# Low halves of converted float64 weights: from GpSimd to VectorE, in one operation with the factor

## The chip, the cores and the metric

The kernel runs on one core of a Trainium2 chip. The engines are called by short names: PE is the matrix engine (PEld its weight loads), DVE the VectorE, ACT the ScalarE, POOL the GpSimd, SP the SyncE, which here only issues transfers. The metric is the device time of one execution in microseconds (us). L1159 is line 1159 of the kernel.

## The reference, cut to what matters

Three layers in a row: attention over a window of 128 keys, a layer of eight experts with one expert per token, and a dense layer with three products whose maximum is taken. The dense layer is the one whose weights the change touches; its inputs stand in float64 in memory.

```python
def reference(**kwargs):
    attn_out = _attn_ref(**attn_kwargs)          # 4 x 8 heads x 576 x 64, window 128
    x = np.ascontiguousarray(attn_out.transpose(0, 2, 1, 3)).reshape(B * S, H * D)
    x = _moe_ref(x=x, **moe_kwargs)              # 2304 x 512, 8 experts, 512 -> 1024 -> 512
    return _moe2_ref(x=x, **moe2_kwargs)

def _moe2_ref(x, w1, w2, w3, w_out) -> np.ndarray:     # 512 -> 768 -> 512
    h = np.maximum(np.maximum(x @ w1, x @ w2), x @ w3)
    return (h @ w_out).astype(np.float32)
    ...
    'w1': np.random.randn(d_model, d_ff).astype(np.float32) * (1.0 / np.sqrt(d_model))
```

The factor `1.0 / np.sqrt(d_model)` is what makes the four weights of the last layer float64.

## The kernel before, in words

**Numbers in halves.** Every operand of a product is held as a float16 high half and a float16 low half (the value minus its high half), and every product is three matmuls: high by high, high by low, low by high (`PASSES`). So each weight needs two conversions: one that writes the high half and one that writes the low half.

**Stages.** The tokens are handled in two halves of 1152. Attention runs first; while it still runs, `layer1(0)` and `layer1(1)` start: the expert layer for the first half, in slots of up to 496, 480 and 224 tokens. The 480 and the 224 slot are `layer1(1)`; they are the last work on PE before the dense layer. Then comes `layer2(0)`, the dense layer for the first half, then `layer1(2)`, `layer1(3)` and `layer2(1)` for the second.

**Weights of the experts** (`Weights`): 8 tiles per expert of 128x1024. A transfer on SP's queue brings one into `st` (L951, three buffers), ACT writes the high half of `wt` (L960), and DVE the low half in one operation with the factor 64 (L969: `st` times `SW` minus `wt`). There are four `wt` buffers; `get(n)` asks for two tiles ahead. In a slot PE runs 24 matmuls on each tile (L997, L1018), ACT empties the sums (L987, L988) and POOL writes the low halves of the results (L989).

**Weights of the dense layer** (`Weights2`): 24 tiles of 128x512 numbers, 18 for `g` (three matrices) and 6 for `wo`. A transfer brings the float64 words into `st2` (L1073, L1079, four buffers). `bits()` makes a float32 out of the two 32-bit words, in three DVE operations, one per `tick()`: L1113, L1117, L1122, into one of five `b64` buffers. `finish()` then makes the halves: ACT multiplies by 64 in place (L1142), ACT writes the high half (L1143), POOL subtracts it and writes the low half (L1144).

**What sets the order.** All instructions stand in the order in which the Python code issues them, per engine; nothing reorders them. In `layer1` the loop adds up the share of time that each step leaves free, and each time the sum passes `TICK` (0.9) it calls one `tick()`; `settled()` calls `finish()` for tiles that are `AGE` (2) ticks old. `tick()` does nothing while more than three tiles wait for their halves. In `layer2`, `inner` calls `convert(3 * m + 3)` before each group m of three products and then two ticks ahead of each product (four where the conversion is less than two groups ahead). One product is 12 matmuls of 384 columns (L1159); ACT (L1166) or DVE (L1168) empties it into `hx`, which has four buffers, as the sums in PSUM have. POOL writes the low half of the maximum (L1188). `outer` does the last product (L1202) with `wo`.

Of the kernel before, what the change touches and what calls it, by code (L numbers as in the profile page):

```python
# [7 lines left out]
F32 = mybir.dt.float32  # L8
# [3 lines left out]
ACTF = mybir.ActivationFunctionType  # L12
ALU = mybir.AluOpType
# [18 lines left out]
KD, KF, K2 = DM // 128, FF // 128, F2 // 128  # L32
SV = 256.0
SX = 64.0
SW = 64.0
# [2 lines left out]
PACE = 0.7  # L38
EXTRA = 2
FILLS = 2  # L40
TICK = 0.9
NG = 2
WAIT = 3
PLACES = 2
# [2 lines left out]
AGE = 2  # L47
# [3 lines left out]
def windowed_attention_moe_kernel(  # L51
# [16 lines left out]
    nc = tc.nc  # L68
# [158 lines left out]
    class Fill:  # L227
# [20 lines left out]
        def finish(self):  # L248
            while self.gens:
                self()  # L250
# [4 lines left out]
    class Attention:  # L255
# [127 lines left out]
        def high(self, ehl):  # L383
            for _, a, b in ehl[2]:
                nc.scalar.activation(out=b, in_=a, func=ACTF.Copy)  # L385
# [480 lines left out]
    class Gather:  # L866
# [22 lines left out]
        def place(self, n=1):  # L889
            for _ in range(n):  # L890
                if not self.q:
                    return
                xg, t, early = self.q.pop(0)
                if early:
                    ps = psM.tile([128, KD, 128], F32, name="m", tag="m")
                    for kk in range(KD):
                        nc.tensor.transpose(ps[:, kk, :], xg[:, 128 * kk:128 * kk + 128], ident)
                    o = self.xT[:, :, :, 128 * t:min(128 * t + 128, self.xT.shape[3])]
                    ps = ps[:, :, 0:o.shape[3]]
                    nc.scalar.activation(out=o[:, 0], in_=ps, func=ACTF.Copy)  # L900
                    nc.vector.tensor_tensor(out=o[:, 1], in0=ps, in1=o[:, 0], op=ALU.subtract)
                    self.sent += 1
                    continue
                xc = self.tile([128, 2, DM], F16, "xc")
                nc.scalar.activation(out=xc[:, 0], in_=xg, func=ACTF.Copy)
                nc.vector.tensor_tensor(out=xc[:, 1], in0=xg, in1=xc[:, 0], op=ALU.subtract)
                self.out.append((xc, t))
# [144 lines left out]
    class Weights2:  # L1052
# [36 lines left out]
        def convert(self, upto):  # L1089
            while self.done < min(upto, self.n):  # L1090
                self.tick()
            while self.half and self.half[0][0] < upto:
                self.finish()

# [9 lines left out]
        def bits(self):  # L1104

            n = self.done
            self.issue(n + 1)
            st = self.st.pop(n).rearrange("p (a two) -> p a two", two=2)  # L1110
            lo, hi = st[:, :, 0], st[:, :, 1]
            b = self.pool.tile([128, 512], I32, name="b64", tag="b64", bufs=B64)
            nc.vector.tensor_scalar(  # L1113
                b, hi, 0x07FFFFFF, 3, ALU.bitwise_and, ALU.logical_shift_left
            )
            yield
            nc.vector.scalar_tensor_tensor(  # L1117
                out=b, in0=lo, scalar=29, in1=b, op0=ALU.logical_shift_right, op1=ALU.bitwise_or
            )
            self.issue(n + ST2)  # L1120
            yield
            nc.vector.scalar_tensor_tensor(  # L1122
                out=b, in0=hi, scalar=-0x40000000, in1=b, op0=ALU.bitwise_and, op1=ALU.bitwise_or
            )
            self.half.append((n, b.bitcast(F32), self.age))
            self.done += 1

        def settled(self):

            while self.half and self.age - self.half[0][2] >= AGE:  # L1130
                self.finish()

        def finish(self):
            if not self.half:
                return
            n, b, _ = self.half.pop(0)
            if n < 3 * K2:
                m, i = divmod(n, 3)
                dst = [self.g[:, l, i, m].rearrange("p k c -> p (k c)") for l in range(2)]
            else:  # L1140
                dst = [self.wo[:, l, n - 3 * K2] for l in range(2)]
            nc.scalar.activation(out=b, in_=b, func=ACTF.Copy, scale=SW)  # L1142
            nc.scalar.activation(out=dst[0], in_=b, func=ACTF.Copy)  # L1143
            nc.gpsimd.tensor_tensor(out=dst[1], in0=b, in1=dst[0], op=ALU.subtract)  # L1144

    C2 = 384

# [168 lines left out]
    with tc.manual_schedule():  # L1316
# [104 lines left out]
        def layer1(u):  # L1421
            nonlocal acc, free
            i = 0
            for c, dv in moe(mw, wst, u, xT[u], yT[u // 2], wait):
# [15 lines left out]
                if w2s:  # L1440
# [6 lines left out]
                    w2s.settled()  # L1447
                    while free > TICK:
                        free -= TICK
                        w2s.tick()  # L1450
# [70 lines left out]
```

## Time and profile before

| | us |
|---|---|
| median of three runs (lowest, highest) | 690.82 (690.08, 690.99) |
| the profiled execution | 690.42 |
| its span, first to last instruction | 688.6 |
| PE busy | 642.8 (93%) |
| DVE busy | 364.4 (53%) |
| ACT busy | 347.0 (50%) |
| POOL busy | 225.2 (33%) |

The profile is of one execution. A busy time is the sum over the whole span, so an engine with 53% can be full in one stretch and idle in another; the slices and stretches show which. A "wait" row names the engine that stood idle, the engine and line that ended the idle time, and the total, the number and the longest of such waits. All the matmuls of the dense layer on the first half lie between 293 and 440 us, those of the 480 and the 224 slot between 232 and 293 us.

### The profile page before, as it was taken

The numbers are of one execution on the slowest core, as the hardware profiler recorded it, in microseconds if no ns is written. First come the engines' busy times: TensorE is split into PE (matmuls) and PEld (weight loads), VectorE is DVE, ScalarE is ACT, GpSimd is POOL, SyncE is SP. The second block draws the span as 40 slices with busy tenths as digits, with TensorE's granted clock in tenths as the row PEclk, the third lists the DMA queues.
The fourth block names the chain that finished last, engine by engine and source line by source line (L and its number), as shares of the span: only waits on it lengthen the run. The fifth ranks groups of instructions, "written<-read, shape, count | busy, mean of one in ns | idle before, by whom it ended". The sixth has DMA issues, their size and how long they took to land.

```text
span 688.6 us, 12881 instructions
## 1 busy us (share of the span) xinstructions
PE 642.8 (93%) x4787; PEld 399.7 (58%) x4787; DVE 364.4 (53%) x1083; ACT 347.0 (50%) x660; POOL 225.2 (33%) x232
## 2 busy tenths in 40 slices
PE   6899889989989997899899999999999999999993
PEld 5687755666657545755564564444448666656641
DVE  5977875865567599999922223152224455201100
ACT  5898887887757365854423211454647211111110
POOL 2111226343112255756534212472424111121121
PEclk9999999999999999999999999999999999999997
DMA  9655773455312665674323403343330000000011
GB/s 192 109 124 134 192 202 82 119 148 152 96 47 66 206 202 163 210 245 161 106 60 82 93 17 123 122 141 104 100 115 2 1 0 1 1 32 17 1 46 49
DMA packets 120800, 69.95 MB, mean 102 GB/s; under 512 B 68872, under 2 KB 115484, under 8 KB 120732
## 3 DMA queue, kind: packets, MB, share of 16 engines
q1 hardware_dynamic: 116992, 59.06, 32.2%
q0 software_dynamic: 3040, 9.96, 4.5%
q8 instruction: 40, 0.66, 0.4%
q14 instruction: 28, 0.23, 0.1%
q10 hardware_dynamic: 700, 0.04, 0.1%
HBM read 57.19 MB, written 9.44 MB: 97 GB/s over the span
## 4 chain that ended last, share of the span: by engine, by line
PE 70%; DVE 15%; ACT 8%; issue 3%; DMA 2%; POOL 1%; POOLq 0%; DVEq 0%; ACTq 0%; SPq 0%
PE m L1159 28%; PE m L1018 10%; PE m L997 10%; PE m L1202 9%; PE s L338 3%; PE m L471 2%; DVE wt L969 2%; PE m L379 2%; PE m L286 2%; ACT e L360 2%; DVE b L1117 2%; DVE e L351 2%; DVE b L1113 2%; PE bank L409 2%; ACT eh L385 1%
## 5 line engine op out<-in xcount | busy, mean ns | idle before, releaser
L1159 PEld LDWEIGHTS <-g 128*128 128x128 f16 x1296 | 126.7, 98 | 87.6 <-issue 4.3
L1159 PE MATMUL m<-yT,g 128*128 128x384 f16 x648 | 106.8, 326 | 2.5 <-DVE hx L1168 1.5
L969 DVE SCALAR_TENSOR_TENSOR wt<-st,wt 128x1024 f16<-128x1024 f32 x48 | 64.3, 1341 | 79.3 <-ACT wt L960 79.3
L1159 PE MATMUL m<-yh,g 128*128 128x384 f16 x648 | 105.7, 327 | 0.0
L1018 PE MATMUL m<-ht,wt 128*128 128x496 f16 (+3 forms) x576 | 102.3, 334 | 3.0 <-DVE wt L969 3.0
L1168 DVE SCALAR_TENSOR_TENSOR hx<-m,hx 128x384 f32<-128x384 f32 x72 | 39.7, 555 | 123.5 <-PE m L1159 120.9
L997 PEld LDWEIGHTS <-wt 128*128 128x128 f16 x576 | 55.8, 100 | 49.8 <-DVE wt L969 4.9
L989 POOL TENSOR_TENSOR ht<-hf,ht 128x496 f16<-128x496 f32 (+3 forms) x48 | 51.0, 1068 | 88.5 <-ACT ht L988 82.8
L1018 PEld LDWEIGHTS <-wt 128*128 128x128 f16 x576 | 54.1, 98 | 43.1 <-DVE wt L969 3.7
L360 ACT ACTIVATE e<-e,nm 128x256 f32<-128x256 f32 (+2 forms) x144 | 59.2, 471 | 27.4 <-DVE nm L351 27.0
L987 ACT ACTIVATE hf<-m 128x496 f32<-128x496 f32 (+3 forms) x72 | 35.9, 498 | 64.7 <-PE m L1018 31.9
L997 PE MATMUL m<-xT,wt 128*128 128x496 f16 (+2 forms) x288 | 59.5, 353 | 6.0 <-DVE wt L969 3.9
L997 PE MATMUL m<-xh,wt 128*128 128x496 f16 (+1 forms) x288 | 51.2, 330 | 0.0
L351 DVE CUSTOM_DVE_ANT_0 e<-s,bias 128x256 f32<-128x256 f32 (+1 forms) x128 | 45.8, 381 | 10.1 <-ACT e L360 4.8
L960 ACT ACTIVATE wt<-st 128x1024 f16<-128x1024 f32 x48 | 49.9, 1044 | 1.0 <-DMA st<-in_moe_w_dram 0.9
L390 DVE TENSOR_TENSOR el<-m,eh 128x512 f16<-128x512 f32 x64 | 42.2, 681 | 9.6 <-ACT eh L385 9.6
L1188 POOL TENSOR_TENSOR xh<-hx,xh 128x384 f16<-128x384 f32 x18 | 16.5, 914 | 89.8 <-ACT xh L1187 89.8
L338 PE MATMUL s<-kT,qT 64*128 64x256 f32 (+2 forms) x320 | 42.4, 386 | 3.3 <-DVE nm L351 2.2
L1187 ACT ACTIVATE xh<-hx 128x384 f16<-128x384 f32 x18 | 9.4, 523 | 71.1 <-DVE hx L1168 67.1
L314 POOL TENSOR_TENSOR vl<-rawv,vh 128x512 f16<-128x512 f32 (+1 forms) x20 | 22.5, 1125 | 65.2 <-ACT vh L307 65.2
L1208 ACT ACTIVATE ob<-m,gate 128x512 f32<-128x512 f32 x18 | 12.4, 687 | 55.0 <-PE m L1202 49.6
L385 ACT ACTIVATE eh<-m 128x512 f16<-128x512 f32 x64 | 34.7, 586 | 4.9 <-PE m L379 4.7
(184 smaller groups left out, 987.4 us busy)
## 6 DMA issues: line engine op xcount, KB each, us to landing
st<-in_moe_w_dram SPq DMA_DIRECT2D x66, 512.0 KB, 3.9
rawk<-in_k_dram SPq DMA_DIRECT2D x16, 256.0 KB, 4.3
rawq<-in_q_dram SPq DMA_DIRECT2D x16, 256.0 KB, 4.8
rawv<-in_v_dram SPq DMA_DIRECT2D x16, 256.0 KB, 4.0
xs<-x SPq DMA_DIRECT2D x16, 256.0 KB, 2.2
st<-in_moe_w_out_dram SPq DMA_DIRECT2D x6, 512.0 KB, 3.4
rawk<-in_k_dram SPq DMA_DIRECT2D x4, 128.0 KB, 5.5
rawq<-in_q_dram SPq DMA_DIRECT2D x4, 128.0 KB, 3.7
```

The lines of the kernel that those rows point to most:

```text
L338: nc.tensor.matmul(out=out[u][rows, x // 2, c0:c1], lhsT=self.qT[b, t][r, i, 0:n], rhs=self.kT[b][r, i, k0 + c0:k0 + c1], start=True, stop ...
L351: nc.vector.tensor_tensor_reduce(out=e[:, x, c0:c1], in0=s[x % 2][:, x // 2, c0:c1], in1=bias[:, x, c0:c1], scale=-0.125, scalar=3.0e38, o ...
L360: nc.scalar.activation(out=e[:, x, c0:c1], in_=e[:, x, c0:c1], func=ACTF.Exp, scale=-1.0, bias=nm[:, x:x + 1],)
L385: nc.scalar.activation(out=b, in_=a, func=ACTF.Copy)
L390: nc.vector.tensor_tensor(out=o, in0=a, in1=b, op=ALU.subtract)
L960: nc.scalar.activation(out=wt[:, 0], in_=st, func=ACTF.Copy, scale=SW)
L969: nc.vector.scalar_tensor_tensor(out=wt[:, 1], in0=st.rearrange("p (a b) -> p a b", a=a), scalar=SW, in1=wt[:, 0], op0=ALU.mult, op1=ALU.s ...
L989: nc.gpsimd.tensor_tensor(out=lo, in0=hf, in1=hi[1], op=ALU.subtract)
L997: nc.tensor.matmul(out=ps, lhsT=wt[:, wl, kk, o:o + 128], rhs=xT[:, xl, kk, bass.ds(d[0], cap)], start=(n == 0), stop=(n == 3 * KD - 1),)
L1018: nc.tensor.matmul(out=ps, lhsT=wt[:, wl, f, :], rhs=hs[f][:, xl], start=(n == 0), stop=(n == 3 * KF - 1),)
L1159: nc.tensor.matmul(out=ps, lhsT=w.g[:, wl, i, m, kk, :], rhs=yT[:, xl, kk, c:c + n2], start=(n == 0), stop=(n == 3 * KD - 1),)
L1202: nc.tensor.matmul(out=ps, lhsT=hm[:, xl, f, 128 * u:128 * u + 128], rhs=w.wo[:, wl, f, :], start=(n == 0), stop=(n == 3 * K2 - 1),)
```

## The change

`finish()` no longer scales on ACT and no longer uses POOL. A new `high()` writes the high half on ACT straight from the float32 tile, with the factor 64 in the same operation. The low half is one DVE operation (`b` times 64 minus the high half), of the same kind as L969. High and low are now two steps: `settled()` writes the high half of every tile that is 2 ticks old, starts its age anew, and writes the low half 2 ticks later. `convert()` calls `settled()` after each tick. `TICK` goes from 0.9 to 1.1.

```diff
-TICK = 0.9
+TICK = 1.1
...
             while self.done < min(upto, self.n):
                 self.tick()
+                self.settled()
...
-            self.half.append((n, b.bitcast(F32), self.age))
+            self.half.append([n, b.bitcast(F32), self.age, False])
...
-            while self.half and self.age - self.half[0][2] >= AGE:
+            for a in self.half:
+                if not a[3] and self.age - a[2] >= AGE:
+                    self.high(a)
+                    a[2] = self.age
+            while self.half and self.half[0][3] and self.age - self.half[0][2] >= AGE:
                 self.finish()
...
+        def high(self, a):
+            nc.scalar.activation(out=self.place(a[0])[0], in_=a[1], func=ACTF.Copy, scale=SW)
+            a[3] = True
...
-            nc.scalar.activation(out=b, in_=b, func=ACTF.Copy, scale=SW)
-            nc.scalar.activation(out=dst[0], in_=b, func=ACTF.Copy)
-            nc.gpsimd.tensor_tensor(out=dst[1], in0=b, in1=dst[0], op=ALU.subtract)
+            a = self.half.pop(0)
+            if not a[3]:
+                self.high(a)
+            hi, lo = self.place(a[0])
+            nc.vector.scalar_tensor_tensor(
+                out=lo, in0=a[1], scalar=SW, in1=hi, op0=ALU.mult, op1=ALU.subtract
+            )
```

In the changed kernel the lines further down have other numbers: L1113, L1117 and L1122 are L1114, L1118 and L1123, L1168 is L1181, and the new operation on DVE is L1155. PE's order stays as it is.

The first place is DVE in the 480 slot, around the third and fourth of the dense layer's tiles that are converted there (`b` is the float32 tile, `st` its words, `wt` an expert's weight). Before:

```order
L1117 SCALAR_TENSOR_TENSOR b_4096<-st_3980,b_4096 128x512
L969 SCALAR_TENSOR_TENSOR wt<-st,wt 128x1024
L1122 SCALAR_TENSOR_TENSOR b_4096<-st_3980,b_4096 128x512
L1113 TENSOR_SCALAR b_4133<-st_3982 128x512
L792 COPY r_eb_4141<-bank 128x1
L1117 SCALAR_TENSOR_TENSOR b_4133<-st_3982,b_4133 128x512
L1122 SCALAR_TENSOR_TENSOR b_4133<-st_3982,b_4133 128x512
```

And in the changed kernel:

```order
L1114 TENSOR_SCALAR b_4110<-st_3980 128x512
L969 SCALAR_TENSOR_TENSOR wt<-st,wt 128x1024
L1155 SCALAR_TENSOR_TENSOR g<-b_3996,g 128x512
L1118 SCALAR_TENSOR_TENSOR b_4110<-st_3980,b_4110 128x512
L792 COPY r_eb_4134<-bank 128x1
L1123 SCALAR_TENSOR_TENSOR b_4110<-st_3980,b_4110 128x512
```

The same piece of DVE's order now holds a low half of an earlier tile, and the conversions stand later. From the first L1113 to the last L969 of the 224 slot the order before has 10 each of L1113, L1117 and L1122; the changed one has 8 each, and 6 of the new operation. Behind that it has 16 tiles to convert and 16 low halves ahead of the last L1123, where 14 tiles stood; the last 2 low halves stand behind it.

The second place is POOL in the 480 and the 224 slot, as a difference:

```order
-L1144 TENSOR_TENSOR g<-b_3996,g 128x512
 L989 ISA
 L989 TENSOR_TENSOR yT_749<-hf,yT_749 128x480
-L1144 TENSOR_TENSOR g<-b_4026,g 128x512
 L989 ISA
 L989 TENSOR_TENSOR yT_749<-hf,yT_749 128x480
-L1144 TENSOR_TENSOR g<-b_4096,g 128x512
-L1144 TENSOR_TENSOR g<-b_4133,g 128x512
```

All 24 rows of L1144 go from POOL's order; what stays there is the expert results' low halves (L989), and in the dense layer those of the maximum (L1188).

The third place is DVE where the conversions of the dense layer end and `outer` is near. In the changed kernel:

```order
L1181 SCALAR_TENSOR_TENSOR hx<-m,hx 128x384 x8
L906 TENSOR_TENSOR xc<-xg,xc 128x512 x2
L1155 SCALAR_TENSOR_TENSOR wo<-b_5151,wo 128x512
L1155 SCALAR_TENSOR_TENSOR wo<-b_5187,wo 128x512
L906 TENSOR_TENSOR xc<-xg,xc 128x512 x2
L1181 SCALAR_TENSOR_TENSOR hx<-m,hx 128x384 x4
```

The low halves of the last two `wo` tiles are issued when `outer` starts, behind two splits of gathered tokens (L906); before, one such tile was left for POOL at that place.

## Rows read from the trace of the kernel before

**Rows 1.** The page: busy tenths of PE and DVE in 40 slices.

```profile
PE   6899889989989997899899999999999999999993
DVE  5977875865567599999922223152224455201100
```

**Rows 2.** Three stretches: length, busy (count) per engine, PEclk, DMA share, GB/s.

```profile
core 0: us, PE busy (x) PEld busy (x) DVE busy (x) ACT busy (x) POOL busy (x), PEclk, DMA share, GB/s
236.00:293.00 57.00, 50.08 (x368) 32.94 (x367) 55.73 (x108) 39.03 (x67) 35.30 (x28) 0.96 0.65 208
293.00:342.90 49.90, 47.36 (x287) 27.80 (x285) 48.14 (x60) 25.04 (x46) 29.55 (x26) 1.00 0.57 174
342.90:372.00 29.10, 28.05 (x168) 16.20 (x166) 9.11 (x16) 8.10 (x16) 10.94 (x11) 1.00 0.25 56
```

**Rows 3.** PE's waits from 236 to 372.5: total us, times, longest.

```profile
PE m L997 <- DVE wt L969: 3.6, 1, 3.6
PE m L1018 <- DVE wt L969: 3.0, 3, 1.5
PE m L1159 <- DVE hx L1168: 1.5, 2, 0.9
PE m L1202 <- POOL wo L1144: 1.0, 1, 1.0
PE m L1159 <- ACT hx L1166: 0.7, 2, 0.5
```

**Rows 4.** DVE in order of time: start us, us, line, operation.

```profile
246.91 1.53 DVE L1117 SCALAR_TENSOR_TENSOR b<-st,b 128x512 int32<-128x512 int32 x1
...
252.34 0.69 DVE L1117 SCALAR_TENSOR_TENSOR b<-st,b 128x512 int32<-128x512 int32 x1
...
291.03 1.53 DVE L1122 SCALAR_TENSOR_TENSOR b<-st,b 128x512 int32<-128x512 int32 x1
...
295.58 1.53 DVE L1122 SCALAR_TENSOR_TENSOR b<-st,b 128x512 int32<-128x512 int32 x1
...
309.06 4.16 DVE L1117 SCALAR_TENSOR_TENSOR b<-st,b 128x512 int32<-128x512 int32 x1
...
341.36 1.53 DVE L1122 SCALAR_TENSOR_TENSOR b<-st,b 128x512 int32<-128x512 int32 x1
```

**Rows 5.** POOL in order of time, at the first and third of these.

```profile
246.54 1.34 POOL L1144 TENSOR_TENSOR g<-b,g 128x512 f16<-128x512 f32 x1 [0.88 <-DVE r_rhs L729]
...
290.65 1.36 POOL L1144 TENSOR_TENSOR g<-b,g 128x512 f16<-128x512 f32 x1 [1.68 <-ACT g L1143]
```

**Rows 6.** Single operations: duration ns min/median/max, first and last start us, forms.

```profile
L1113 DVE TENSOR_SCALAR b<-st x24: 406/420/1727, 236.6 to 338.6; 128x512 int32<-128x512 int32 x24
L1117 DVE SCALAR_TENSOR_TENSOR b<-st,b x24: 671/693/4156, 237.3 to 339.8; 128x512 int32<-128x512 int32 x24
L906 DVE TENSOR_TENSOR xc<-xg,xc x10: 679/684/1050, 322.8 to 394.2; 128x512 f16<-128x512 f32 x10
L1142 ACT ACTIVATE b<-b x24: 612/615/633, 245.1 to 368.1; 128x512 f32<-128x512 f32 x24
```

**Rows 7.** L1144 on POOL in the first two stretches of rows 2.

```profile
236.00:293.00 57.00, 14.25 (x9) 0.96 0.65 208
293.00:342.90 49.90, 17.18 (x14) 1.00 0.57 174
```

**Rows 8.** PE in order of time, a stretch of 204 matmuls.

```profile
333.27 33.74 PE L1159 MATMUL m<-yT,g 128*128 128x384 f16 x204 [0.66 <-DVE hx L1168]
```

**Rows 9.** Two stretches around PE's longest wait (columns as in rows 2).

```profile
267.30:270.88 3.58, 0.00 (x0) 0.07 (x1) 3.55 (x4) 2.08 (x5) 2.11 (x3) 1.00 0.28 94
270.90:274.30 3.40, 3.40 (x19) 2.70 (x20) 3.40 (x7) 0.75 (x2) 0.37 (x1) 0.50 0.58 169
```

**Rows 10.** The page: ACT's high halves of the experts' weights, idle before them.

```profile
L960 ACT ACTIVATE wt<-st 128x1024 f16<-128x1024 f32 x48 | 49.9, 1044 | 1.0 <-DMA st<-in_moe_w_dram 0.9
```

**Rows 11.** A later stretch (columns as in rows 2).

```profile
400.00:450.00 50.00, 50.00 (x267) 25.20 (x265) 13.85 (x31) 13.83 (x23) 16.59 (x15) 1.00 0.29 93
```

More of the change, by code (lines that the diff above doesn't have):

```diff
@@ L1124, in bits, with place @@
             )
-            self.half.append((n, b.bitcast(F32), self.age))
+            self.half.append([n, b.bitcast(F32), self.age, False])
             self.done += 1
         def settled(self):
-            while self.half and self.age - self.half[0][2] >= AGE:
-                self.finish()
+            for a in self.half:
[3 more added lines that the diff above has]
+            while self.half and self.half[0][3] and self.age - self.half[0][2] >= AGE:
+                self.finish()
+        def place(self, n):
+            if n < 3 * K2:
+                m, i = divmod(n, 3)
+                return [self.g[:, l, i, m].rearrange("p k c -> p (k c)") for l in range(2)]
+            return [self.wo[:, l, n - 3 * K2] for l in range(2)]
+        def high(self, a):
+            nc.scalar.activation(out=self.place(a[0])[0], in_=a[1], func=ACTF.Copy, scale=SW)
+            a[3] = True
         def finish(self):
@@ L1135, in finish @@
                 return
[L1136 to L1141, printed above, removed]
-            nc.scalar.activation(out=b, in_=b, func=ACTF.Copy, scale=SW)
-            nc.scalar.activation(out=dst[0], in_=b, func=ACTF.Copy)
-            nc.gpsimd.tensor_tensor(out=dst[1], in0=b, in1=dst[0], op=ALU.subtract)
+            a = self.half.pop(0)
[5 more added lines that the diff above has]
+            )
     C2 = 384
```

## The prediction, made before the changed kernel ran

> **What bounds the kernel now.** I read the slices first: PE is at eight or nine tenths nearly everywhere, and DVE, half idle over the span, stands at nine tenths in a block from the slice at 240 us to that at 340 [rows 1]. So the question is whether PE waits for DVE there. The stretches say that DVE is the fuller of the two: 55.73 of 57 us in the stretch of the 480 and 224 slots (A, 236 to 293), 48.14 of 49.9 in the first part of the dense layer (B, 293 to 342.9), and only 9.11 of 29.1 behind it (C) [rows 2]. PE's waits in A to C name DVE for most of what they hold: 3.6 and 3.0 us for L969 in A, 1.5 for L1168 in B; there are also 0.7 for ACT in B and 1.0 for L1144 itself where `outer` begins [rows 3]. That is 9.8 us. Behind it PE is busy 50.00 of 50 us [rows 11], so what PE gets back before 372 reaches the end unshortened.
>
> Why is DVE full? L1117 takes 0.69 us at 252.34, but 1.53 at 246.91 and L1122 1.53 at 291.03 [rows 4]. At each of the slow ones POOL had started a row of L1144 a little earlier (246.54, 290.65) [rows 5], and the DVE operation ends within its own 0.69 us of POOL's end (248.44 after 247.88): it is held up until POOL is nearly through. Followed one by one through the two timelines, 9 DVE operations in A stand behind a row of L1144, one for each of its 9 rows there [rows 7]; the first is at 246.91, the last at 291.03, each about 0.85 us too long, 7.9 us in all. In B, 11 operations stand behind L1144 alone, from 295.58 to 341.36 [rows 4], 8.6 us in all; two more stand behind a chain of POOL work in which L1144 has a part. The larger is at 309.06, 4.16 us instead of 0.69 [rows 4]; of the 4.8 us of the two I give L1144 3.3, its part of those chains' time on POOL. Together 7.9 in A and 11.9 in B.
>
> **The change part by part.**
>
> *ACT* loses 24 operations of 0.615 us [rows 6]. It is busy 39 of 57 us in A and 25 of 49.9 in B [rows 2], and PE waited for it 0.7 us [rows 3]. I credit nothing; if ACT were the next bound this would be a gain. *POOL* loses 24 operations, whose only direct cost to PE is the 1.0 us at `outer` [rows 3]. *SP* gets two transfers of float64 words fewer ahead of the last expert weights in A, and one `wo` transfer behind two transposes for gathered tokens. These tokens are used in the slots after the dense layer, some 50 us later; nothing is charged, and without that cover it would be a few us at the start of `layer1(2)`.
>
> *The new operation* (L1155) reads 128x512 float32 and float16 from SBUF and writes float16. The row of that very form is L906, 0.68 us, with L1117 of the same width at 0.67 to 0.69 [rows 6]. The next operation starts a little before the end of the one ahead, so I take 0.65. A conversion is 0.42 + 0.69 + 0.69, 1.8 us [rows 6]; L1122, which has no row there, is read as L1117, of the same form.
>
> *A, in DVE's time.* Two conversions leave (10 become 8): -3.6. Six low halves come: 6 x 0.65 = +3.9. The waits behind L1144 go: -7.9. The new operations, with two inputs in SBUF like L1117, will themselves stand behind L989 at times: POOL's other work is 35.30 - 14.25 = 21 of 57 us [rows 2, 7], so a hit for one in three at about half of 0.85, 0.2 each, +1.1; the six operations that leave take as much with them. The sum is -7.6. PE cannot get back more than it waited in A, 6.6 us [rows 3], and not all of that, since the 224 slot wants a tile of weights every 2 to 3 us and DVE is still over eight tenths full: I take -6.0. The bounds: if the next POOL row took over half of the holding up, 3.9 of the 7.9 would stay, -3.6 and as much for PE, or -1.5 if the remaining work falls badly; at the other end all 6.6, and a little more. For after the longest wait, in which PE did nothing for 3.58 us, the granted clock is 0.50 for 3.40 us, with 19 matmuls [rows 9]; that is the 1.2 GHz level. Without the wait that could go too, 1.7 us at most. I don't count it, because DVE ends later than PE there anyway. So -8.3 to -1.5.
>
> *B, in DVE's time.* Two conversions come (14 become 16): +3.6. Sixteen low halves: +10.4. Contention of the 22 new operations with the 29.55 - 17.18 = 12.4 us of POOL that stay [rows 2, 7]: about +2.7. Gone: -11.9. So DVE has 4.8 us more to do in B. Yet the pace counts, and it is set by code: two ticks for a product, three ticks a conversion, so one conversion for 1.5 products. A product is 12 of the matmuls of which 204 take 33.74 us [rows 8], 1.98 us, so a conversion has 2.97 us. Before, DVE used 48.14 / 14 = 3.44 for each, all its other work included, and fell behind by 14 x 0.47 = 6.6 us; four buffers of `hx` and of the sums took up 4.4 of it and PE waited the remaining 2.2 [rows 3]. Now it is (48.14 + 4.8) / 16 = 3.31, and it falls behind by 16 x 0.34 = 5.4, less 4.4 is 1.0 for PE. So -1.2. The bounds: no lag beyond the buffers, -2.2; 4 us less relief than I read, 9.4 - 4.4 = 5.0, which is +2.8. The tiles themselves are no risk: a low half is written tens of us before its product (the conversions end at 342.9, matmuls on `g` run until 367 [rows 4, 8]).
>
> *C.* The 1.0 us for L1144 at `outer` goes. In its place two low halves stand on DVE behind two L906 of 0.68 [rows 6]; they are needed at the 14th and 17th matmul, some 3 us in. I take -0.7, between -1.0 and +1.0.
>
> The sum: -6.0 - 1.2 - 0.7 = -7.9, on the profiled execution's own 690.42: 682.5. That execution lies 0.4 under the median of 690.82, so for a median **682.9**, 1.1% faster.
>
> **The rivals.**
>
> *Weights become the bound in A.* With DVE freed, a tile of expert weights still has to come by transfer and pass ACT (1.04 us) with three buffers; ACT waited 0.9 us for such transfers already [rows 10], while DVE was late. If this takes PE's waits in A over, only half of the 6.0 comes: 690.8 - 3.0 - 1.2 - 0.7 = **685.9**. For it: there are such waits while ACT is idle for a third of A [rows 2]. Against: in the 480 slot a tile lasts PE 5 us, and the early buffers come free earlier too.
>
> *Everything goes.* No wait is left in A to C and the slow clock goes with them: 690.8 - 9.8 - 1.7 = **679.3**. For it: in B the lag is near what the buffers hold. Against: DVE stays the fullest engine.
>
> *DVE overloaded: slower.* The stretching isn't L1144's alone to give back; L989 and L1188, or POOL's transfers, take its places, and 22 low halves (14.3 us) come on top of a full engine. With no relief, A is -3.6 + 3.9, nothing; in B DVE has 48.14 + 16.7 = 64.8 us for 16 conversions, 4.05 each against 2.97, a lag of 17.3, and PE waits 17.3 - 4.4 = 12.9 where it waited 2.2: 690.8 + 10.7 = **701.5**. It decides from the point where about half of the relief stays away (10.7 - 11.9r - 7.5r = 0 at r = 0.55). For it: DVE at 98% [rows 2] takes work from an engine at 60%. Against: L1144 stands beside the slow operations one for one, and POOL's other rows stay as many as they were. The Trainium skill, on the page "Perfetto Trace Analysis", section "Optimizing Scalar/DVE Operations", says that where DVE is saturated, moving work from it to Scalar or even GPSIMD may make sense, and this change goes the other way; by that sentence alone it is this rival that comes. The same paragraph adds that moving work between DVE and GPSIMD might not help, as they share a port; the rows bear out that half, with 0.85 us for one meeting.
>
> *It changes nothing:* DVE's time in A is replaced by waits for transfers to the full. I see too few of these in [rows 10].
>
> **How the numbers follow.** Forecast (680.2 to 685.4) 0.65; weights bound 0.16; everything goes 0.10; slower 0.06; nothing 0.03. The first two and most of the third make the range: 679.3 to 687.0 leaves out the upper part of the weights' case, the last two cases and a little at the bottom. What a measurement here can tell from no change is about 0.2%, 1.4 us. Faster by more 0.91, within 0.03, slower by more 0.06.
>
> **What would show it.** In the changed profile, L1117 and L1122 (there L1118 and L1123) near 0.69 in the median, with fewer long ones; the sum of PE's waits for L969 under 2 us; the first dense product about 6 us earlier than 293; in B waits for `hx` of 1 us or less; the new operation near 0.68. I would be wrong if long conversions stay as many with L989 or L1188 beside them, if the waits for L969 become waits for ACT or transfers, or if PE's waits for `hx` grow to several us.

## The result and the profile after

The changed kernel takes 679.86 us in the median of 4 runs (678.68 to 685.38), the kernel before 690.45 beside it. The ratio is 0.984, 95% interval 0.981 to 0.988: 10.6 us or 1.6% faster. That is 3.0 us below the predicted time, inside its range (679.3 to 687.0) and just below the 680.2 at which the forecast's own case began. The profiled execution took 680.68 us with a span of 678.8.

First the slices of the page after, to be held against [rows 1]. Of PE's digits two have changed, the seven at 258 us and the eight at 327, which are nines now, and DVE is as full there as it was:

```profile
PE   6899889989989999899999999999999999999993
...
DVE  6977865866567599999923331252224355101100
```

PE's waits from 225 to 372 us answer to [rows 3] (total, times, longest). Of the 9.8 us there, one wait of 2.8 for L969, 0.5 at the first product and 0.5 where `outer` begins are left, and none for `hx`:

```profile
PE m L1018 <- DVE wt L969: 2.8, 1, 2.8
...
PE m L1172 <- POOL yT L989: 0.5, 1, 0.5
PE m L1215 <- DVE wo L1155: 0.5, 1, 0.5
```

The single operations on DVE answer to [rows 6] (ns minimum/median/maximum). Both steps of a conversion stand at 0.69 in the median; the longest L1117 was 4.16 us and is 1.94 now. The new operation is near 0.68:

```profile
L1118 DVE SCALAR_TENSOR_TENSOR b<-st,b x24: 669/684/1943, 238.9 to 336.1; 128x512 int32<-128x512 int32 x24
L1123 DVE SCALAR_TENSOR_TENSOR b<-st,b x24: 670/686/1472, 239.6 to 337.8; 128x512 int32<-128x512 int32 x24
L1155 DVE SCALAR_TENSOR_TENSOR g<-b,g x18: 674/684/1526, 248.8 to 324.3; 128x512 f16<-128x512 f32 x18
```

**Where the time went.** Executions differ by up to 4.6 us before the first conversion: PE's first product for an expert starts at 96.8 us before, at 97.1 after, and between 96.8 and 101.4 in the other kernels. So I measure two stages between marks on PE. A' runs from the first product of the 480 slot's second layer (242.82 before, 242.13 after) to the first dense product; B' from there to the first product of `outer`. In both, all these kernels run the same matmuls. The columns are those of [rows 2]. A' before, A' after, and A' after in another execution of the changed kernel:

```profile
242.82:292.98 50.16, 43.24 (x336) 29.73 (x335) 49.61 (x88) 35.73 (x62) 32.01 (x26) 0.97 0.62 195
```

```profile
242.13:286.69 44.56, 41.71 (x336) 28.88 (x334) 42.95 (x96) 27.84 (x51) 23.76 (x17) 1.00 0.65 206
```

```profile
243.13:286.10 42.97, 41.65 (x335) 28.87 (x334) 42.15 (x91) 28.97 (x51) 21.64 (x17) 1.00 0.67 212
```

A' is 5.6 us shorter, 7.2 in the other execution. Length less PE's busy time is what PE waited: 6.92 before, 2.85 and 1.32 after. The busy time itself fell by 1.5 us for the same matmuls. That is the clock, 0.97 over the stage before and 1.00 after: the stretch at 0.50 behind the longest wait [rows 9] is gone. B' before and after:

```profile
292.98:366.84 73.86, 71.32 (x434) 42.20 (x432) 55.51 (x72) 31.06 (x59) 36.16 (x33) 1.00 0.44 132
```

```profile
286.69:357.64 70.95, 70.43 (x434) 42.26 (x433) 55.09 (x92) 24.14 (x48) 19.10 (x19) 1.00 0.54 148
```

B' is 2.9 us shorter: 2.0 of waits and 0.9 of busy time. Behind B', up to the last product of `outer`, it is 0.6 us, and ahead of A' 0.7. The last is luck of the execution: the granted clock is 0.50 from 233.4 to 236.8 us before and 1.00 there after, but in another execution of the changed kernel (`after_third` below) it is 0.52 at the same place. -5.6 - 2.9 - 0.6 - 0.7 = -9.8, the difference of the spans.

### The profile page after: what moved, and what is told of

It is laid out like the page before. It is cut to its first block, busy times and chain, and to the rows that moved or that the text cites. A ratio compares the mean times of both kernels' runs of the same rounds, so it can differ in the third digit from the quotient of the medians.

```text
span 678.8 us, 12834 instructions
## 1 busy us (share of the span) xinstructions
PE 639.0 (94%) x4787; PEld 399.6 (59%) x4787; DVE 358.3 (53%) x1107; ACT 331.3 (49%) x636; POOL 198.6 (29%) x208
## 4 chain that ended last, share of the span: by engine, by line
PE 78%; DVE 8%; ACT 8%; DMA 3%; issue 1%; POOL 1%; POOLq 0%; ACTq 0%; DVEq 0%
PE m L1172 31%; PE m L1018 13%; PE m L997 11%; PE m L1215 9%; PE s L338 4%; PE m L379 2%; PE m L471 2%; PE m L286 2%; ACT e L360 2%; PE bank L409 2%; DVE e L351 2%; ACT eh L385 2%; DMA xg<-xs,r_gidx 1%; DVE wt L969 1%; DVE el L390 1%
## 5 line engine op out<-in xcount | busy, mean ns | idle before, releaser
L969 DVE SCALAR_TENSOR_TENSOR wt<-st,wt 128x1024 f16<-128x1024 f32 x48 | 62.7, 1307 | 80.6 <-ACT wt L960 80.5
L1018 PE MATMUL m<-ht,wt 128*128 128x496 f16 (+3 forms) x576 | 101.8, 333 | 2.8 <-DVE wt L969 2.8
L1181 DVE SCALAR_TENSOR_TENSOR hx<-m,hx 128x384 f32<-128x384 f32 x72 | 40.0, 556 | 121.6 <-PE m L1172 121.5
L997 PEld LDWEIGHTS <-wt 128*128 128x128 f16 x576 | 54.3, 97 | 44.8 <-ACT wt L960 1.8
L1018 PEld LDWEIGHTS <-wt 128*128 128x128 f16 x576 | 54.2, 98 | 42.4 <-DVE wt L969 3.3
L989 POOL TENSOR_TENSOR ht<-hf,ht 128x496 f16<-128x496 f32 (+3 forms) x48 | 51.5, 1081 | 82.2 <-ACT ht L988 78.8
L997 PE MATMUL m<-xT,wt 128*128 128x496 f16 (+2 forms) x288 | 56.2, 335 | 2.7 <-ACT wt L960 1.6
L960 ACT ACTIVATE wt<-st 128x1024 f16<-128x1024 f32 x48 | 49.9, 1044 | 1.6 <-DMA st<-in_moe_w_dram 1.5
L1201 POOL TENSOR_TENSOR yh<-hx,yh 128x384 f16<-128x384 f32 x18 | 18.1, 1003 | 79.0 <-ACT yh L1200 79.0
```

Source lines behind the costliest of these rows:

```text
L960: nc.scalar.activation(out=wt[:, 0], in_=st, func=ACTF.Copy, scale=SW)
L969: nc.vector.scalar_tensor_tensor(out=wt[:, 1], in0=st.rearrange("p (a b) -> p a b", a=a), scalar=SW, in1=wt[:, 0], op0=ALU.mult, op1=ALU.s ...
L989: nc.gpsimd.tensor_tensor(out=lo, in0=hf, in1=hi[1], op=ALU.subtract)
L997: nc.tensor.matmul(out=ps, lhsT=wt[:, wl, kk, o:o + 128], rhs=xT[:, xl, kk, bass.ds(d[0], cap)], start=(n == 0), stop=(n == 3 * KD - 1),)
L1018: nc.tensor.matmul(out=ps, lhsT=wt[:, wl, f, :], rhs=hs[f][:, xl], start=(n == 0), stop=(n == 3 * KF - 1),)
L1181: nc.vector.scalar_tensor_tensor(out=nx, in0=ps, scalar=2.0 ** -6, in1=run, op0=ALU.mult, op1=ALU.max)
```

## The experiments

Four comparisons were made, each with its own runs of the kernel before: medians 694.2, 690.5, 695.3 and 690.6 us. So times are compared as ratios to before; "set to 690.45" is the ratio times that number, for the expectations. PE's wait is A' less its busy time there. A' and B' are each of one profiled execution; the three of the changed kernel differ by 1.7 us in A' and by nothing in B'.

```
kernel            median  ratio [95%]            A'     PE wait  PEclk  B'
before            690.5   1                      50.16  6.92     0.97   73.86
changed           679.9   0.984 [0.981, 0.988]   44.56  2.85     1.00   70.95
after_again       679.8   0.984 [0.980, 0.988]   44.70  3.00     1.00   70.95
after_third       680.9   0.987 [0.984, 0.990]   42.97  1.32     1.00   70.95
e1_move_only      693.8   0.998 [0.995, 1.001]   49.31  4.67     0.93   73.75
e2_no_move        688.5   0.990 [0.987, 0.994]   47.55  4.97     1.00   70.55
e3_act_kept       679.5   0.985 [0.980, 0.989]   43.63  1.98     1.00   70.99
e4_pool_again     704.2   1.013 [1.010, 1.017]   48.49  4.82     0.96   82.80
e5_pool_memset    691.0   0.994 [0.992, 0.997]   45.76  2.92     0.96   74.96
e6_no_low         682.8   0.984 [0.981, 0.987]   43.74  1.86     1.00   70.62
e7_two_lows       693.1   1.003 [1.000, 1.006]   46.26  3.33     0.96   78.72
e8_three_hf       681.3   0.985 [0.981, 0.989]   44.41  2.61     1.00   70.95
e9_tick_13        684.9   0.986 [0.981, 0.990]   42.91  1.21     1.00   70.50
e10_tick_13       679.3   0.983 [0.980, 0.986]   42.91  1.19     1.00   70.50
```

Theory 1 is the prediction's: POOL's L1144 held DVE up, and its going is the gain. Theory 2 is the move of two conversions behind A by TICK. Theory 3 is the operation saved on ACT.

One more count serves them: the DVE operations of the conversions (the three steps, and the low half where DVE writes it) that took over 1.2 us. There are 21 before, 8 in the changed kernel, 15 in e1, 17 in e4, 10 in e5 and 4 in e6.

**The move alone** (e1, on the kernel before).

```diff
-TICK = 0.9
+TICK = 1.1
```

> The kernel before with one number changed, TICK 1.1 in place of 0.9, so that conversions come later; high and low halves stay as they were, on ACT and POOL. Theory 1 (hold-ups: the gain is DVE no longer standing behind POOL's L1144): two conversions leave A with their hold-ups, 2 x 1.8 + 2 x 0.85 = 5.3 us of DVE time, and the rest of the hold-ups stays; at most about half of the measured 10.6 us comes, 685 to 689, and some 18 to 22 long conversions remain. Theory 2 (the move: the gain is only that two conversions leave the full stretch A): all of it comes, 679 to 682.

Set to 690.45 it is 689.1: nothing that can be told from no change. Theory 2 is out as the whole cause, and theory 1 was too generous with the move: it had 685 to 689, and 18 to 22 long operations where 15 are left. PE's wait in A' did fall, from 6.92 to 4.67, but B' stayed and the clock took most of that back (0.93). One of the two waits left in A' has a new name, `PE m L1018 <- POOL ht L989`, 2.8 us. POOL in order of time there shows why:

```profile
280.49 2.35 POOL L1144 TENSOR_TENSOR g<-b,g 128x512 f16<-128x512 f32 x1
282.80 5.18 POOL L989 TENSOR_TENSOR ht<-hf,ht 128x224 f16<-128x224 f32 x2
```

L989 took 0.61 us at 276.60; here two take 5.18, behind an L1144 that itself took 2.35 and not 1.34 [rows 5]. DVE ran L1122, L969, L1113, L969 and L1117 end to end from 283.63 to 287.50 meanwhile. POOL is held up as well as DVE.

**The low halves alone** (e2, on the changed kernel).

```diff
-TICK = 1.1
+TICK = 0.9
```

> The changed kernel with one number put back, TICK 0.9, so that 10 conversions stay in A; low halves on DVE, one ACT operation, nothing on POOL. Theory 1 (hold-ups), by the prediction's account: in A the 9 hold-ups go (-7.9), 8 low halves come (+5.2) with hits of their own (+1.3), so DVE gains 1.4 us there, B 0.5 and outer 0.7: 686 to 689. If the hold-ups alone were the whole gain, without help from the move: 680 to 682. Theory 2 (the move): no gain, 689 to 692, or slower by the added 14 us of DVE work.

Set to 690.45 it is 683.7, between the two forms of theory 1: two thirds of the gain without the move. B' is already at 70.55; in A' PE still waits 4.97 us, since 10 conversions with their low halves fill DVE there. Move and low halves take 2.25 and 1.95 us of PE's wait in A' each by itself. Together they take 4.1 in the changed kernel's first profile and 5.6 in its third, so whether they simply add up isn't shown.

**POOL's subtraction put back beside the changed kernel** (e4).

```diff
+            t = self.pool.tile([128, 512], F16, name="extra", tag="extra", bufs=2)
+            nc.gpsimd.tensor_tensor(out=t, in0=a[1], in1=hi, op=ALU.subtract)
```

> The changed kernel, and after each low half POOL does the same subtraction once more into a scratch tile that nobody reads, so that 24 operations like L1144 stand on POOL again beside DVE. This adds work and changes no result. Theory 1 (hold-ups): DVE is held up again, 24 times about 0.85 us, while it also does the low halves; most of the gain goes, 686 to 695, and long conversions (over 1.2 us) are back to some 20. Theory 2 (the move) and theory 3 (the saved ACT operation): POOL's work is beside the point, 679 to 682.

It is 1.3% slower than before, 699.5 when set to 690.45, past what theory 1 gave (686 to 695), with 17 long operations (some 20 expected). DVE's own waits there name PE and ACT and never POOL, so it isn't a buffer kept by the added operation that delays DVE. This is the rival "DVE overloaded" built by hand: the low halves on DVE and no relief, priced at 10.7 us over before; measured 9.1. One meeting, first POOL, then DVE:

```profile
307.27 1.15 POOL L1159 TENSOR_TENSOR extra<-b,g 128x512 f16<-128x512 f32 x1 [2.08 <-ACT g L1145]
```

```profile
307.30 1.67 DVE L1118 SCALAR_TENSOR_TENSOR b<-st,b 128x512 int32<-128x512 int32 x1
```

DVE's operation, started 0.03 us later, takes 1.67 and not 0.68, and ends 0.55 after POOL's. PE then waits for `hx` through the dense layer (total, times, longest), and B' is 82.80 with DVE at 68.03:

```profile
PE m L1174 <- DVE hx L1183: 7.5, 8, 2.9
```

```profile
296.22:379.02 82.80, 73.81 (x434) 42.78 (x433) 68.03 (x92) 23.50 (x47) 37.99 (x34) 0.98 0.42 123
```

**No low halves at all** (e6, on the kernel before; PE reads the high halves in their place).

```diff
-            nc.gpsimd.tensor_tensor(out=dst[1], in0=b, in1=dst[0], op=ALU.subtract)
...
-                        out=ps, lhsT=w.g[:, wl, i, m, kk, :],
+                        out=ps, lhsT=w.g[:, 0, i, m, kk, :],
```

> The kernel before without L1144: the low halves of the converted weights are not computed at all, and the matmuls that would read them read the high halves instead, so there are as many of them. Left out is the correction by the low halves. TICK stays 0.9 and ACT keeps both operations. Theory 1 (hold-ups): DVE is relieved of 19.8 us and gets no work for it, so this gives at least what the change gives without its move, 680 to 684; conversions are near 0.69 us. Theory 2 (the move): no gain, 689 to 691. Theory 3 (the saved ACT operation): no gain, 689 to 691.

Set to 690.45: 679.3. With the old TICK and both ACT operations, taking L1144 away brings the whole gain. The stage rows, A' and B':

```profile
245.52:289.26 43.74, 41.88 (x335) 28.80 (x334) 41.16 (x89) 35.13 (x62) 17.93 (x17) 1.00 0.70 224
```

```profile
289.26:359.88 70.62, 70.36 (x434) 42.27 (x433) 41.53 (x71) 31.60 (x60) 18.38 (x19) 1.00 0.47 138
```

Against e2, which has the low halves on DVE as well, B' is the same to 0.1 us although DVE has 10 us less to do (41.53 against 51.39), and A' is 3.8 us shorter. So the low halves cost nothing on DVE in B', and 3.8 us in A' if no conversion is moved out of it (one profile of each; the medians, 682.8 and 688.5, are 5.7 apart). That is what the change's TICK is there to pay for.

**The operation on ACT kept** (e3, against the changed kernel).

```diff
-            nc.scalar.activation(out=self.place(a[0])[0], in_=a[1], func=ACTF.Copy, scale=SW)
+            nc.scalar.activation(out=a[1], in_=a[1], func=ACTF.Copy, scale=SW)
+            nc.scalar.activation(out=self.place(a[0])[0], in_=a[1], func=ACTF.Copy)
...
-            nc.vector.scalar_tensor_tensor(
-                out=lo, in0=a[1], scalar=SW, in1=hi, op0=ALU.mult, op1=ALU.subtract
-            )
+            nc.vector.tensor_tensor(out=lo, in0=a[1], in1=hi, op=ALU.subtract)
```

> The changed kernel, but ACT scales the tile in place again ahead of the high half, as before (24 more operations of 0.615 us), and DVE's low half is a plain subtraction of the same width. The move and the place of the low halves stay. Theory 1 (hold-ups) with the prediction's account, which credited ACT's relief with nothing: within 1 us of the changed kernel. Theory 3 (the saved ACT operation): ACT's delay goes on to the high halves of the experts' weights (L960) and PE's wait for L969 grows: 2 to 5 us slower than the changed kernel.

Beside it stood the changed kernel itself:

> The changed kernel itself, on the same chip as the runs beside it, so that they can be set against it. All theories: 0.981 to 0.988 of the kernel before.

679.5 against 679.8 us, with A' 43.63 and B' 70.99. The 2 to 5 us of theory 3 are neither in the medians nor in the stages: ACT's relief is worth nothing that can be told, as credited.

**Every low half twice** (e7: after L1155 the same operation once more, into a scratch tile).

```diff
+            nc.vector.scalar_tensor_tensor(
+                out=t, in0=a[1], scalar=SW, in1=hi, op0=ALU.mult, op1=ALU.subtract
+            )
```

> The changed kernel with every low half computed twice on DVE, the second time into a scratch tile that nobody reads: 24 more operations of about 0.65 us, work that changes no result. It measures what a microsecond of DVE costs here. The prediction's account of B (DVE falls behind its pace already): 10.4 us more in B and 3.9 in A reach PE nearly whole, 12 to 16 us slower than the changed kernel. Rival (DVE keeps up in B with something to spare, 2.5 us idle in the first part of the dense layer and 4.4 of buffers): 5 to 9 us slower.

By the medians 13.2 us slower than the changed kernel beside it; the stages of the one profile have 1.7 in A', 7.8 in B' and 0.6 behind. The prediction's account is right in kind: past a point DVE's time goes to PE nearly whole. B':

```profile
289.50:368.22 78.72, 71.75 (x434) 42.20 (x433) 63.95 (x108) 23.54 (x47) 18.50 (x18) 1.00 0.44 130
```

DVE is busy 8.9 us longer than in the changed kernel's B' and the stage is 7.8 longer. By that the changed kernel has about 1 us of room there; e9 below puts 1.2 us more on DVE in B' (56.26) and the stage is no longer for it (70.50).

**POOL busy, but without reading** (e5: 24 memsets on POOL beside the changed kernel).

```diff
+            t = self.pool.tile([128, 1300], F16, name="extra", tag="extra", bufs=1)
+            nc.gpsimd.memset(t, 0.0)
```

> The changed kernel, and after each low half POOL writes zeros to a scratch tile of 128x1300 that nobody reads: 24 operations more on POOL of about the length of L1144 (an estimate: 1.3 us), which write and read nothing. Work is added and no result changed. If any busy POOL holds DVE up, as in the run with the second subtraction: 692 to 705, and 25 or more long DVE operations. If it takes a POOL operation that reads two inputs beside DVE's: 678 to 683, and long DVE operations stay near 14.

It is 686.5 when set to 690.45, in neither range, and the trace says which operations suffer. Four memsets stand in a row on POOL, 1.17 to 1.34 us each; beside them, DVE:

```profile
297.75 5.21 POOL L1159 MEMSET extra<- 128x1300 f16 x4
```

```profile
297.25 1.95 DVE L1114 TENSOR_SCALAR b<-st 128x512 int32<-128x512 int32 x1
299.24 0.69 DVE L1118 SCALAR_TENSOR_TENSOR b<-st,b 128x512 int32<-128x512 int32 x1
299.85 0.68 DVE L1155 SCALAR_TENSOR_TENSOR g<-b,g 128x512 f16<-128x512 f32 x1
300.45 0.69 DVE L1123 SCALAR_TENSOR_TENSOR b<-st,b 128x512 int32<-128x512 int32 x1
301.05 0.79 DVE L1114 TENSOR_SCALAR b<-st 128x512 int32<-128x512 int32 x1
```

The one-input L1114 is held up. The first one began under an L989 (296.85 to 297.81) and was held through the first memset as well, 1.95 us and not 0.42; with memsets alone it took 0.66 to 0.93 in six meetings, and ended 0.28 us after the memset each time. The two-input operations run at their own length: 20 of them began while a memset ran, and the longest took 0.69. Before, 18 began under an L1144, and 13 of these took over 1.2. So among the conversions a memset lengthens the one-input step alone (L1114 0.81 us in the mean, 0.47 in the changed kernel), and the two-input operations are held up where POOL's operation is a subtraction, which reads. The Trainium skill, page "SBUF — State Buffer", section "SBUF: two separate sides", says that DVE and GPSIMD share a pair of ports as an exclusive lock, taken by DVE operations in a two-port mode, and by those with two inputs in SBUF only against a GPSIMD operation that reads SBUF. The two traces agree: 0.69 beside a memset, 1.67 beside a subtraction.

**A third buffer for hf** (e8).

```diff
-            hf = pool.tile([128, 512], F32, name="hf", tag="hf", bufs=2)[:, 0:cap]
+            hf = pool.tile([128, 512], F32, name="hf", tag="hf", bufs=3)[:, 0:cap]
```

> The changed kernel with three buffers for hf in place of two. In the changed kernel POOL's L989 was itself held up once by DVE (3.87 us instead of 1.1 at 263.52), ACT's L987 then waited 1.79 us for the buffer, L960 came late behind it, and PE's only long wait in A (2.76 us for L969) followed. If that chain makes the wait: 1 to 2.5 us faster than the changed kernel. If the wait comes from DVE's own queue (the routing operations ahead of L969): within 0.5 us of it.

681.3 against 679.8, A' 44.41: no gain. ACT's wait for the buffer fell from 1.79 to 0.70 us, and the L969 behind it no longer waited for ACT, but PE's wait for a later L969 is still 2.5 us. So the buffer was not what made it. That leaves the other branch, DVE's own queue; the rows for it stand at the end of the next section.

**A later TICK** (e9 and e10, on the changed kernel).

```diff
-TICK = 1.1
+TICK = 1.3
```

> The changed kernel with TICK 1.3 in place of 1.1: 9 conversions before the dense layer in place of 10, one more in it. From the run with two low halves, which added 10.4 us to DVE in the first part of the dense layer and cost 7.8 us there, some 2.6 us are spare; one conversion and its low half are about 2.4 us. If the 2.8 us that PE still waits for L969 comes from DVE's queue: 1 to 2.5 us faster than the changed kernel. If the spare time isn't there: 0 to 2 us slower, with waits for hx in the dense layer.

> The changed kernel once more, beside the one with TICK 1.3 on the same chip. All theories: 0.981 to 0.988 of the kernel before.

> The changed kernel with TICK 1.3 a second time, now beside the changed kernel on the same chip, since the first time they stood in different comparisons. By its first profile the stretch from the first product of the 480 slot's second layer to the first product of the dense layer is 42.9 us (changed kernel 44.6) and the dense layer's first part 70.5 (70.95): 1.5 to 2.5 us faster than the changed kernel if that holds in the whole time; no difference if it is lost behind them.

Both profiles have 42.91 in A' and 70.50 in B'. But A' of the changed kernel is 44.56, 44.70 or 42.97 from one execution to the next, and in the last of these there is nothing left to gain in A'. Side by side the medians are 679.25 and 680.94, with overlapping intervals (0.980 to 0.986, 0.984 to 0.990). e9's ratio, 0.986 beside 0.984 to 0.987 for the changed kernel, shows no gain. It may be 1 to 2 us faster; that isn't settled.

## Why the prediction came out as it did

**The bound and its cause: right.** DVE was the late engine and L1144 held it up. e6 shows it (the whole gain from taking L1144 away), and e4 the other way round (all of it lost, and more, from putting such an operation back). The long operations went from 21 to 8. POOL's own load is not what PE waited for: its waits for POOL before are 0.2 us in the dense layer and the 1.0 at `outer`, and 0.3 in e5 with as many operations on POOL again. Of the signs named, the first dense product (286.69), the medians near 0.69, the new operation at 0.68 and no wait for `hx` came; PE's waits for L969 under 2 us didn't (2.8, 2.9 and 1.3 in three profiles).

**The number: inside the range, partly by luck.** By the profiles -7.9 was forecast and -9.8 found. A' gave 0.4 less than forecast, B' 1.7 more, C 0.1 less, and 0.7 lies ahead of A' and belongs to the execution. The forecast's own case, 680.2 to 685.4, was missed by 0.3 us.

**A: the size is right, the make-up isn't.** Predicted -6.0, found -5.6 in A' (-7.2 in the other execution). DVE's time was forecast to fall by 7.6; its busy time in A' fell by 6.7. But PE's waits gave only 4.1 of the 5.6 in the profiled execution (5.6 of 7.2 in the other), so that -6.0 nearly came is partly luck: the other 1.5 is the clock, which the prediction saw in [rows 9] and left out, "because DVE ends later than PE there anyway". That step failed: PE's busy time fell from 43.24 to 41.71. Where both kernels ran side by side, the mean granted clock over the span was 0.986 or more in 5 of 28 executions of the kernel before and in 7 of 12 of the changed one: stretches at the lower clock are rarer after the change and not gone for good. I can't tell when one comes. The changed kernel has a wait of 2.76 us in A' and stays at 1.00; e4 has one of 2.73 and the granted clock is 0.51 behind it.

**B: this term was mis-sized, outside its own bounds.** Predicted -1.2 (from -2.2 to +2.8), found -2.9. Two steps failed. The first is DVE's time. In the part with conversions the prediction had 48.14 + 4.8 us for 16 of them, 3.31 each; the profile after has 49.25, or 3.08:

```profile
286.70:338.50 51.80, 51.28 (x317) 30.74 (x315) 49.25 (x83) 18.81 (x37) 12.51 (x12) 1.00 0.66 183
```

Less holding up was left than forecast. The three steps of the conversions grouped, in the first part of the dense layer (busy us, mean ns), before:

```profile
L1117 DVE SCALAR_TENSOR_TENSOR b<-st,b 128x512 int32<-128x512 int32 x14 | 15.5, 1106 | 0.2
L1122 DVE SCALAR_TENSOR_TENSOR b<-st,b 128x512 int32<-128x512 int32 x14 | 14.8, 1059 | 0.4
L1113 DVE TENSOR_SCALAR b<-st 128x512 int32<-128x512 int32 x14 | 11.0, 784 | 0.0
```

and after:

```profile
L1118 DVE SCALAR_TENSOR_TENSOR b<-st,b 128x512 int32<-128x512 int32 x16 | 12.2, 764 | 0.3
L1123 DVE SCALAR_TENSOR_TENSOR b<-st,b 128x512 int32<-128x512 int32 x16 | 11.3, 705 | 0.3
L1155 DVE SCALAR_TENSOR_TENSOR g<-b,g 128x512 f16<-128x512 f32 x12 | 10.0, 837 | 0.0
...
L1114 DVE TENSOR_SCALAR b<-st 128x512 int32<-128x512 int32 x15 | 7.1, 471 | 0.0
L1155 DVE SCALAR_TENSOR_TENSOR wo<-b,wo 128x512 f16<-128x512 f32 x4 | 3.5, 863 | 0.0
```

That is 41.3 us for 14 conversions and 30.6 for 16, of which one L1114 lies just ahead of the stretch. Less the work itself (1.8 us each, 0.42 less for the missing step), 16.1 us of holding up became 2.2. The 16 low halves took 13.5 us where 0.65 each makes 10.4, so 3.1 came back there. What is left is 5.3 us. The prediction gave 11.9 of the 16.1 to L1144, left the other 4.2 with POOL's other rows and added 2.7 for the new operations: 6.9. These 1.6 us and the 0.4 of the L1114 ahead are 2.0 of the 3.7 by which DVE was overestimated (52.9 against 49.25); the rest I have not itemised. With the prediction's own pace and buffers, 16 x (3.08 - 2.97) = 1.8 is less than the 4.4 that the buffers hold, so no wait is left, and none was.

The second step is the 2.2 us that PE could get back. In [rows 3] that is the sum of the listed waits for `hx`. Over B' PE was idle for 2.54 us, in seven pauses, and for the same 434 matmuls at clock 1.00 it was also 0.89 busy longer than after, where there is one pause. In the trace a matmul lasts 0.326 us and the next one starts 0.162 after it, so a pause costs about 0.16 us beyond its idle time. Six pauses fewer make 1.0, and 0.89 was found. The other profiles fit: 70.36 us busy with one pause (e6), 70.88 with four (e5), 71.33 with seven (e1), 71.75 with nine (e7). So 2.54 + 0.89 = 3.4 us, and not 2.2, stood to be won, and 2.9 came.

**C: right.** Predicted -0.7, found -0.6: the 1.0 for L1144 became 0.5 for L1155.

**ACT at nothing, POOL's other rows, the tiles:** as said (e3; between 225 and 372 us no wait of PE is for a transfer).

**The rivals.** "Weights become the bound" didn't come: between 225 and 372 us no wait of PE names ACT's L960 or a transfer. "Everything goes" has nearly the measured time (679.3) and half the mechanism: the slow clock and all of B went, but 2.8 us for L969 stayed in A in two of three profiles of the changed kernel (2.8, 2.9, 1.3). "DVE overloaded" needed the relief to stay away; e4 shows its price was fair, 10.7 forecast and 9.1 measured over before. The sentence of the Trainium skill beside it (page "Perfetto Trace Analysis", section "Optimizing Scalar/DVE Operations", on taking work off a saturated DVE) pointed the wrong way here: DVE, at 98% in A, took over low halves from POOL, and even without the move (e2) its busy time in A' fell, from 49.61 to 47.03 us. The other half of that paragraph, on the port that the two share, is the half that e4 and e5 bear out.

**What is left in A.** The changed kernel's wait for L969 is 2.8 us in one execution and 1.3 in another. In the profiled one a POOL operation is late beside DVE's, then ACT behind it, then one L969:

```profile
263.52 3.87 POOL L989 TENSOR_TENSOR yT<-hf,yT 128x480 f32 x1 [2.98 <-ACT yT L988]
...
267.42 0.36 ACT L987 ACTIVATE hf<-m 128x224 f32<-128x224 f32 x1 [1.79 <-POOL yT L989]
...
268.11 1.04 ACT L960 ACTIVATE wt<-st 128x1024 f16<-128x1024 f32 x1
...
269.18 1.23 DVE L969 SCALAR_TENSOR_TENSOR wt<-st,wt 128x1024 f16<-128x1024 f32 x1 [1.25 <-ACT wt L960]
```

But the L969 that PE waits for is the next one:

```profile
270.32 0.33 DVE L614 TENSOR_SCALAR r_pos<-r_pos,past 128x1 f32<-128x1 f32 x2
270.39 1.04 ACT L960 ACTIVATE wt<-st 128x1024 f16<-128x1024 f32 x1
...
275.61 0.38 DVE L752 SCALAR_TENSOR_TENSOR r_le<-r_le,r_end 1x8 f32<-1x8 f32 x1
...
275.92 1.21 DVE L969 SCALAR_TENSOR_TENSOR wt<-st,wt 128x1024 f16<-128x1024 f32 x1
...
277.18 1.04 PE L1018 MATMUL m<-ht,wt 128*128 128x224 f16 x9 [2.76 <-DVE wt L969]
```

Its high half was there at 271.43, and DVE started it at 275.92. In between DVE ran the routing operations (L614 to L752) and one L1118 that stand ahead of it in the order, 5.6 us end to end. So the wait is made by DVE's own queue, the second branch of e8. In the execution with 1.3 us (two waits) the same queue takes 5.1 us and starts earlier; why it starts earlier there stays open.

## What to carry to other kernels

Where DVE is the full engine, look for POOL operations that start just ahead of its long ones: an operation that moves from POOL to DVE can leave DVE with less to do, since here 24 subtractions on POOL cost DVE more than doing them itself (its busy time over the span fell from 364.4 to 358.3 us). A move of work that only shifts load between stages could not be told from nothing before the relief (0.998); with it the ratio went from 0.990 to 0.984, by intervals that just touch. So try such numbers (TICK) after the relief, and not instead of it. To size the relief, sum the holding up over all operations of a stage (here 16.1 us of 41.3), and say which part of it is given to which cause. Count the pauses too, and not only their listed idle time.

## What the runs showed of the hardware

- The holding up goes both ways. One L989 of 128x480, 1.08 to 1.88 us at the three other places in that slot, took 3.87 us beside operations that DVE ran end to end, and two of 128x224 took 5.18 (e1), where one had taken 0.61.
- Which DVE operation suffers depends on what POOL does: beside memsets the one-input L1114 took 0.66 to 0.93 us in six meetings and not 0.42, and all 20 two-input operations at most 0.69; beside a subtraction the two-input L1118 took 1.67, ending 0.55 after it.
- With the same 434 matmuls at clock 1.00, PE's busy time was 70.4 us with one pause, 70.9 with four (4.1 us idle) and 71.3 with seven (2.5 us idle): about 0.16 us for each pause, whatever its length.
- A wait of PE of 2.73 us was followed by a stretch at clock 0.51 (e4), and one of 2.76 was not (changed kernel).
